# One PSUM pool with numbered accumulators for an MLP and a recurrence, and an accumulator of its own for the second transposed norm

## Chip, cores, metric

The kernel runs on one core of one Trainium2 chip. The metric is device time in microseconds (us), lower is better; beside it stands the span of the profiled execution, from its first to its last instruction.

## The reference, cut to what matters

Two computations on the same `x` (2048 rows of 512) are mixed by a gate that depends on the row:

```python
g = sigmoid((x * gate_w).sum(-1, keepdims=True))
a = A_ref(x, mem0, Wq, Wk, Wv, Wo, seg_len)   # 64 segments of 32 rows, in sequence: each attends to
                                              # 8 memory rows that the segment before it produced
b = gelu(layernorm(x) @ w1 + b1) @ w2 + b2    # MLP 512 -> 1376 -> 512, no recurrence
out = g * a + (1 - g) * b
```

## The kernel before

It computes the MLP first (until 99.7 us), keeps `(1 - g) * b` in on-chip memory, and then runs the 64 steps of the recurrence. The kernel uses eight banks of PSUM, the memory into which its matmuls write. An eviction copies a finished result out of its bank, on VectorE or ScalarE. The MLP takes the banks from two pools, the recurrence from a third that is opened when the MLP's pools are closed:

```python
mps = mlp.enter_context(tc.tile_pool(name="mps", bufs=1, space=PSUM))       # tp, hp x2, bp0..bp3: 7 banks
pools = {"ps": mlp.enter_context(tc.tile_pool(name="pre", bufs=1, space=PSUM)), ...}   # b5: 1 bank
def bank(k, shape, dtype=FP32):
    return pools["ps"].tile(shape, dtype, tag=f"b{k}", name=f"b{k}")

def norm_tr(T, y_sb):                              # transposes a normalized tile of x
    tp = mps.tile([P, KC, P], BF16, tag="tp", name="tp")
    for kc in range(KC):
        nc.tensor.transpose(tp[:, kc, :], y_sb[:, kc * P:(kc + 1) * P], ident[:])
    nc.vector.tensor_copy(out=yTs[blk][...], in_=tp[:])
# up(u): hp = mps.tile(tag="hp", bufs=2); GELU on ScalarE.   down(u): bp = mps.tile(tag=f"bp{T % 4}")
# ... cut ...
norm_tr(0, ys[0]); norm_tr(1, ys[1])               # the first two, one behind the other
for u in range(NBLK * FC):                         # 8 blocks of two x tiles, 11 chunks of F each
    ...                                            # up(u), down(u - 2), norms of the next block
    if fc == 2: c_act()                            # ScalarE evicts the odd tile of the block before
    if blk % 2 == 0:
        if fc in (2, 5, 6, 7): bn(...)             # statistics of later x tiles, VectorE
        if fc == 8: newton(...)                    # their inverse roots, VectorE
    if blk == 0 and fc in (9, 10): gates(fc - 9, fc - 8)   # x * gate_w, summed, tiles 0 and 1, VectorE
    if blk == 1 and fc == 0: gates2(0, 2)          # tanh on ScalarE
for a in pend: down(*a)
c_act()                                            # the last tile, T = 15
mlp.close()
# ... cut ...
pb = loop.enter_context(tc.tile_pool(name="pb", bufs=1, space=PSUM))        # b0..b7
pools.update(ps=pb, sb=cw, nTt=3, nside=2)
nc.scalar.activation(out=warm[:], in_=g_all[:, 0:1], func=ACTF.Exp)         # loads ScalarE's table
S_next = mask_mm()                                 # 4 matmuls into b7: the first work of the recurrence
```

All of it:

## Time and profile before

| | before |
|---|---|
| device time, median of the first 3 runs | 822.22 us (822.06 to 823.05) |
| profiled span | 821.1 us |
| TensorE busy | 793.0 us, 97% |
| TensorE idle in all | 28.1 us |
| of it in front of the second transposes | 0.52 us |
| of it in front of the first mask matmuls | 0.78 us |

In a timeline row stand the start, the duration, the engine, the source line, the operation, what it writes and reads, and in brackets how long the engine had been idle and what released it. Idle time counts for the end only if the chain of waits runs through it. The rows themselves are in the prediction.

### The profile page before, as it was taken

The numbers are of one execution on the slowest core, as the hardware profiler recorded it, in microseconds if no ns is written. First come the engines' busy times: TensorE is split into PE (matmuls) and PEld (weight loads), VectorE is DVE, ScalarE is ACT, GpSimd is POOL, SyncE is SP. The second block draws the span as 40 slices with busy tenths as digits, with TensorE's granted clock in tenths as the row PEclk, the third lists the DMA queues.
The fourth block names the chain that finished last, engine by engine and source line by source line (L and its number), as shares of the span: only waits on it lengthen the run. The fifth ranks groups of instructions, "written<-read, shape, count | busy, mean of one in ns | idle before, by whom it ended". The sixth has DMA issues, their size and how long they took to land.

```text
span 821.1 us, 48437 instructions
## 1 busy us (share of the span) xinstructions
PE 793.0 (97%) x22013; PEld 443.4 (54%) x22013; DVE 493.1 (60%) x1022; ACT 446.6 (54%) x1239; POOL 272.7 (33%) x624
## 2 busy tenths in 40 slices
PE   6999999999999999999999999999999999999986
PEld 3666545555555555555555555555555555555543
DVE  5764256565656666665666565666566565756554
ACT  3555445655555555555555645555565555565553
POOL 8100224242434243243424242423333242424220
PEclk9999999999999999999999999999999999999999
DMA  9791310000000010101010100101010101010000
GB/s 314 238 404 48 104 28 11 25 16 15 25 20 26 10 36 10 37 11 33 6 38 10 31 17 20 27 18 28 10 36 11 36 4 40 7 34 8 10 5 24
DMA packets 38357, 37.59 MB, mean 46 GB/s; under 512 B 13561, under 2 KB 36578, under 8 KB 36610
## 3 DMA queue, kind: packets, MB, share of 16 engines
q1 hardware_dynamic: 38018, 34.31, 12.6%
q8 instruction: 174, 2.85, 1.5%
q14 instruction: 37, 0.30, 0.1%
q0 software_dynamic: 128, 0.13, 0.1%
HBM read 26.03 MB, written 6.29 MB: 39 GB/s over the span
## 4 chain that ended last, share of the span: by engine, by line
PE 92%; DVE 4%; issue 1%; DMA 1%; SPq 1%; ACT 1%; DVEq 0%; ACTq 0%
PE b L211 33%; PE b L233 18%; PE b L222 16%; PE b L398 5%; PE hp L470 4%; PE bp L487 4%; PE b L360 3%; PE b L374 2%; PE b L365 2%; PE b L383 2%; PE b L403 1%; DVE R L692 1%; DMA Wo_sb<-in_A_x_dram 1%; DVE Pm L695 1%; PE b L387 0%
## 5 line engine op out<-in xcount | busy, mean ns | idle before, releaser
L217 DVE STREAM_TRANSPOSE Tt<-b 128x512 f32<-128x512 f32 (+1 forms) x384 | 225.6, 613 | 82.2 <-PE b L211 70.3
L211 PEld LDWEIGHTS <-hT 128*32 128x32 bf16 x5120 | 131.3, 97 | 108.2 <-DVE hT L721 23.5
L233 PE MATMUL b<-Wo_sb,UTT 128*32 128x512 bf16 (+1 forms) x2656 | 160.9, 378 | 1.3 <-ACT UTT L763 0.9
L222 PE MATMUL b<-Wv_sb,hT 128*32 128x512 bf16 x2048 | 141.8, 378 | 0.0
L211 PE MATMUL b<-Wq_sb,hT 128*32 128x512 bf16 x2048 | 133.3, 380 | 3.2 <-DVE hT L721 1.7
L211 PE MATMUL b<-Wk_sb,hT 128*32 128x256 bf16 (+1 forms) x3072 | 133.3, 308 | 0.0
L667 ACT CAST KT<-Tt 128x256 bf16<-128x256 f32 (+1 forms) x192 | 87.1, 476 | 53.6 <-DVE Tt L217 53.5
L620 POOL TENSOR_TENSOR Px<-E,R 128x256 bf16<-128x256 bf16 x63 | 42.5, 675 | 208.9 <-DVE R L704 208.9
L704 DVE RECIPROCAL R<-b 128x256 f32<-128x256 f32 x63 | 110.7, 1757 | 0.0
L667 POOL CAST QT<-Tt 128x512 bf16<-128x512 f32 x64 | 39.2, 613 | 187.1 <-DVE Tt L217 187.1
L233 PEld LDWEIGHTS <-UTT 128*32 128x32 bf16 x2656 | 64.4, 96 | 63.8 <-DVE UTT L703 12.2
L711 ACT CAST wsb<-b 128x512 bf16<-128x512 f32 x63 | 36.9, 586 | 111.2 <-PE b L233 111.2
L692 DVE RECIPROCAL R<-b 128x64 f32<-128x64 f32 x63 | 35.1, 557 | 78.4 <-PE b L360 78.4
L634 ACT CAST UTT<-b 128x256 bf16<-128x256 f32 x248 | 74.4, 386 | 9.7 <-PE b L403 7.5
L667 ACT CAST QT<-Tt 128x512 bf16<-128x512 f32 x64 | 39.6, 619 | 68.7 <-DVE Tt L217 68.7
L222 PEld LDWEIGHTS <-hT 128*32 128x32 bf16 x2048 | 49.4, 96 | 21.2
L475 ACT ACTIVATE hg<-hp,b_sb 128x256 bf16<-128x256 f32 x80 | 37.8, 474 | 39.9 <-PE hp L470 39.9
L721 DVE CAST hT<-b 128x32 bf16<-128x32 f32 x63 | 12.1, 191 | 79.0 <-PE b L365 79.0
L398 PEld LDWEIGHTS <-V 32*128 32x128 bf16 x4064 | 34.4, 91 | 45.6 <-DVE Pm L695 32.3
L470 PE MATMUL hp<-yT,w_sb 128*128 128x256 bf16 (+1 forms) x352 | 54.7, 281 | 2.2 <-DMA w_sb<-in_B_w_dram 0.9
L703 ACT CAST UTT<-b 128x64 bf16<-128x64 f32 x126 | 20.6, 215 | 66.1 <-PE b L403 66.1
L622 POOL TENSOR_TENSOR racc<-racc,R 128x320 f32<-128x320 f32 x63 | 54.9, 871 | 0.0
(131 smaller groups left out, 1056.5 us busy)
## 6 DMA issues: line engine op xcount, KB each, us to landing
Wv_sb<-in_A_Wv_dram SPq DMA_DIRECT2D x4, 1024.0 KB
Wq_sb<-in_A_Wq_dram SPq DMA_DIRECT2D x4, 1024.0 KB
Wk_sb<-in_A_Wk_dram SPq DMA_DIRECT2D x4, 1024.0 KB
Wo_sb<-in_A_Wo_dram SPq DMA_DIRECT2D x2, 2048.0 KB
vd<-vt SPq DMA_DIRECT2D x32, 128.0 KB
vs<-vd SPq DMA_DIRECT2D x256, 16.0 KB
out_dram<-o SPq DMA_DIRECT2D x15, 128.0 KB
Wo_sb<-in_A_x_dram SPq DMA_DIRECT2D x1, 1024.0 KB
```

The lines of the kernel that those rows point to most:

```text
L211: nc.tensor.matmul(bk[32 * j:32 * j + 32, 0:n], lhsT=G[:, kc, :], rhs=W5[t][:, kc, h0:h1, j, :], start=(kc == 0), stop=(kc == KC - 1), til ...
L217: nc.vector.transpose(out=Tt[:, 0:n], in_=bk[:, 0:n])
L222: nc.tensor.matmul(bk[32 * j:32 * j + 32, :], lhsT=G[:, kc, :], rhs=Wv5[:, kc, 4 * vb:4 * vb + 4, j, :], start=(kc == 0), stop=(kc == KC - ...
L233: nc.tensor.matmul(bk[32 * g:32 * g + 32, :], lhsT=ut[:, i, j, c0:c0 + 32], rhs=Wo_sb[:, 4 * i + j, d0:d1], start=(j == 0 and i < 4), stop ...
L398: nc.tensor.matmul(U[j][:, i, :], lhsT=V[q, i, :], rhs=Pt[q, i, c_main:c_main + n], start=(i == 0), stop=False, skip_group_check=True, til ...
L470: nc.tensor.matmul(hp[:rows, :], lhsT=w1_sb[:, kc, fc * P:fc * P + rows], rhs=yTs[blk][:, kc, :], start=(kc == 0), stop=(kc == KC - 1))
L620: nc.gpsimd.tensor_tensor(out=Px[:, :, 0:32], in0=E[:, :, 16:48], in1=Rr, op=ALU.mult)
L622: nc.gpsimd.tensor_tensor(out=racc[:], in0=racc[:], in1=R[:], op=ALU.add)
L634: nc.scalar.copy(out=UTT[T % 2][:, :, j, c0 + M:c0 + 40], in_=U[:])
L667: (nc.gpsimd.tensor_copy if bi == 2 else nc.scalar.copy)(out=dst, in_=Tv)
L692: nc.vector.reciprocal(out=R[:, 0:8 * NG].rearrange("p (i q) -> p i q", q=8), in_=sm[:])
L704: nc.vector.reciprocal(out=R[:, 8 * NG:].rearrange("p (i q) -> p i q", q=32), in_=sr)
```

## The change

The intent: one pool `pb` lives from the start to the end, and every PSUM tile is one of its numbered accumulators. `hp` becomes b0 and b1, `bp` becomes b2, b3, b4, b6, the side work stays b5, `tp` becomes b7. A tile then waits only for the last user of its own accumulator, not for a whole pool. The second transposed norm goes into b6, which nothing else needs so early, so it need not wait for the copy of the first.

```diff
+    pb = loop.enter_context(tc.tile_pool(name="pb", bufs=1, space=PSUM))
     mlp = ExitStack()
...
-    mps = mlp.enter_context(tc.tile_pool(name="mps", bufs=1, space=PSUM))
-    pools = {"ps": mlp.enter_context(tc.tile_pool(name="pre", bufs=1, space=PSUM)), "sb": mwork}
+    pools = {"sb": mwork}
...
     def bank(k, shape, dtype=FP32):
-        return pools["ps"].tile(shape, dtype, tag=f"b{k}", name=f"b{k}")
+        return pb.tile(shape, dtype, tag=f"b{k}", name=f"b{k}")
...
-    def norm_tr(T, y_sb):
+    def norm_tr(T, y_sb, k=7):
-        tp = mps.tile([P, KC, P], BF16, tag="tp", name="tp")
+        tp = bank(k, [P, KC, P], BF16)
...
-        hp = mps.tile([P, TB * P], FP32, tag="hp", bufs=2, name="hp")
+        hp = bank(u % 2, [P, TB * P])
...
-                bpt[T] = mps.tile([P, Dm], FP32, tag=f"bp{T % 4}", name="bp")
+                bpt[T] = bank((2, 3, 4, 6)[T % 4], [P, Dm])
...
-    norm_tr(1, ys[1])
+    norm_tr(1, ys[1], 6)
...
-    pb = loop.enter_context(tc.tile_pool(name="pb", bufs=1, space=PSUM))
-    pools.update(ps=pb, sb=cw, nTt=3, nside=2)
+    pools.update(sb=cw, nTt=3, nside=2)
```

## The prediction

> **What bounds the kernel now.** I read the page's busy shares first, then the chain of waits in order of time, then the timeline around the two places that the diff touches.
>
> ```profile
> PE 793.0 (97%) x22013; PEld 443.4 (54%) x22013; DVE 493.1 (60%) x1022; ACT 446.6 (54%) x1239; POOL 272.7 (33%) x624
> ...
> PE   6999999999999999999999999999999999999986
> ...
> PE 92%; DVE 4%; issue 1%; DMA 1%; SPq 1%; ACT 1%; DVEq 0%; ACTq 0%
> ```
>
> TensorE is busy for 97% of 821.1 us and carries 92% of the chain that ended last. The row of tenths falls under 9 only in the first slice (0 to 20.5 us) and at the very end. So a change can win only where TensorE stands still and something on the chain holds it; 28 us in all (821.1 - 793.0). Two of those gaps belong to code in the diff. The first is at the start, in the TensorE timeline:
>
> ```profile
> 5.66 0.60 PE L459 MATMUL tp<-ident,y 128*128 128x128 bf16 x4 [5.66 <-DVE y L452]
> 6.78 0.58 PE L459 MATMUL tp<-ident,y 128*128 128x128 bf16 x4 [0.52 <-DVE yT L460]
> 7.88 2.72 PE L470 MATMUL hp<-yT,w_sb 128*128 128x256 bf16 x12 [0.52 <-DVE yT L460]
> 10.39 1.06 PE L487 MATMUL bp<-w_sb,hg 128*128 128x512 bf16 x2
> 12.39 1.04 PE L470 MATMUL hp<-yT,w_sb 128*128 128x256 bf16 x4 [0.94 <-DMA w_sb<-in_B_w_dram]
> ```
>
> The second transposes wait 0.52 us for VectorE to copy the first ones out of the single tp buffer; the third row waits 0.52 us again. The last row waits for a weight transfer. The second gap is where the MLP ends and the recurrence begins, same view:
>
> ```profile
> 99.12 0.60 PE L487 MATMUL bp<-w_sb,hgl 97*128 97x512 bf16 x2
> 100.50 0.37 PE L374 MATMUL b<-MkA,ident 128*32 128x448 bf16 x4 [0.78 <-ACT c_all L495]
> 100.69 1.05 PE L211 MATMUL b<-Wq_sb,hT 128*32 128x512 bf16 x16
> ```
>
> The mask matmuls open the recurrence; their operands are long there, yet they wait 0.78 us until ScalarE has finished the MLP's last eviction. Whether a gap is on the chain, the chain of waits in order of time says:
>
> ```profile
> 8.04 8.09 DMA Wo_sb<-in_A_x_dram
> 16.15 0.70 DVE st L413
> ...
> 24.42 0.47 ACT hg L475
> 24.93 0.60 PE hp L470 x4
> ...
> 98.43 1.31 PE bp L487 x6
> 99.74 0.02 issue
> 99.76 0.70 ACT c_all L495
> 100.46 0.04 issue
> 100.50 0.37 PE b L374 x4
> ```
>
> TensorE enters the chain only at 24.93 us. Before that the chain is the transfer of x tiles (lands at 16.13), then VectorE statistics and gates in queue order, then ScalarE. So the first gap lies off the chain, the second lies on it.
>
> **What the Trainium skill says.** "PSUM — Partial Sum Buffer", section "PSUM bank collisions raise a hardware error": access to PSUM is to be guarded by semaphores per bank (and quadrant). That is why a new owner of a bank waits for the last reader of the old one, which is legitimate; but the wait at 100.50 us is wider: in the built program of before the mask's accumulator lies in bank 0, where the transposes' buffer was, while the evictions at 99.55 and 99.76 us read banks of the MLP's down-projection. The wait is that of a new pool for the whole old pool. "Perfetto Trace Analysis", "Matmuls": independent matmul groups should rotate through different banks so that one's eviction overlaps the next one's matmuls; both gaps here break that, and the trace agrees (0.52 and 0.78 us idle). "ScalarE: Activation LUTs", "What ACT_TABLE_LOAD costs": about 1283 ns for the load; the trace has 1.28 us at 100.51 us. "TensorE: Matmul & The Clock Gate", "What's actually happening": the array starts at half rate and is released after a free-running window of about 3.4 us of activity. The trace agrees in kind: four matmuls of 256 columns take 1.04 us at 12.39 us and 0.60 us from 15.73 us.
>
> **The change part by part.** I compared the two built programs instruction by instruction, line numbers and names set aside. All five engines have the same instructions in the same order (47,729 entries on TensorE), and SBUF addresses are equal. The only differences in waits are five, all on TensorE: the second transposes lose their wait for VectorE; the mask's weight load loses its wait for VectorE and the first mask matmul its wait for ScalarE; the first matmuls into b2 and into b4 in the first step gain a wait each for VectorE. Physical banks are permuted; each accumulator still has one of its own.
>
> (1) Second transposed norm. Both y tiles are ready at 5.19 + 0.73 = 5.92 us. Four cold transposes take about 0.45 us of issue (the weight-load row of that place: 0.45), so the second four can go at about 6.1 us in place of 6.78: 0.68 us earlier. VectorE copies them behind its first copy (6.30 + 0.42), from about 6.73 in place of 7.40; the up-projection starts at about 7.2 in place of 7.88. TensorE then reaches the weight wait at about 10.8 in place of 11.45, and the transfer still comes at 12.38: the 0.94 us wait becomes about 1.6 us. Even without that wait, the chain from 8.04 to 24.42 us holds no TensorE work, and TensorE idles 0.77 us before 24.93 us for ScalarE. Value to the end: 0.
>
> (2) The hand-over of the pools. Two 512-column matmuls issue in 0.43 us (elsewhere in the MLP such a pair is followed by the next group 0.43 us later: 93.92 to 94.35). The pair at 99.12 is therefore issued by 99.55, and the mask can go at 99.55 instead of 100.50: 0.95 us. In later steps the mask follows its predecessor with some 0.2 us of weight-load issue on the load side, about 0.05 of it seen by the matmuls, so 0.9 us.
>
> (3) Does it arrive? The table load for Exp starts at 100.51 us after the last eviction and, with the warm call, holds ScalarE until 101.81 + 0.20 = 102.01 us. The first query cast stands at 102.69, waiting for VectorE; 0.92 us earlier it would be ready at 101.77 and starts 0.24 us late at 102.01. It takes 0.62, so the second (ready at 103.40 - 0.92 = 102.48) starts at 102.63, 0.15 late; the next (104.59 - 0.92 = 103.67) finds ScalarE free since 103.25. The delay is gone before the scores (104.80 before), which waited for no cast anyway. GpSimd's query cast had 1.62 us of idle time ahead. VectorE's first block transpose would move from 101.94 to about 101.0, after the eviction that ends at 100.30.
>
> (4) The two new waits: b4's matmuls come 4 x 0.86 us after the first block's start at about 99.75, so at about 103.2; the last VectorE eviction ended at 100.30. Cost 0. The side accumulator b6 is free since 100.45 and is wanted at about 106.
>
> (5) The remaining 63 steps have the same instructions and waits and move as one block: no further gain or loss.
>
> Sum: 0 + 0.92 + 0 = 0.92 us; 822.22 - 0.92 = 821.3 us, and the profile's span 821.1 - 0.9 = 820.2.
>
> **The rivals.** (A) The start counts too: 0.68 + 0.92 = 1.6 us, 820.6. For it: TensorE really starts earlier, and may leave its half-rate state earlier. Against: the weight wait at 12.39, and the chain, which meets TensorE only at 24.93. (B) ScalarE's table load takes the place of the removed wait: if the first step hung on its casts, 0.24 us of 0.92 would be lost, or all of it if the table load delayed the chain; 821.5 to 822.2. For: it becomes the last thing to end. Against: 0.57 us of idle time ahead of the key cast at 104.59 absorbs it. (C) The clock release falls one 3.4 us window later because TensorE's idle stretch before 12.39 grows. That costs at most about half a window, 1.7 us, less the 0.77 us of slack at 24.93: 822.2. It varies from run to run whatever the kernel. (D) The word-by-word intent (one pool, numbered accumulators) suggests a freer recurrence, several per cent; but its 63 steps have unchanged waits, so I give it next to nothing.
>
> **Range and chances.** The three times of before lie within 822.06 to 823.05, about 1 us, as large as the effect; a median of three should scatter by some 0.5 us. With A at one side and B and C at the other: 820.4 to 822.4 us. Two per cent would be 16.4 us, over half of all TensorE's idle time: faster 0.005, same 0.99, slower 0.005.
>
> **What would show it.** Right: the transposes at about 6.1 us without a wait; the weight wait grown to about 1.6 us; the 24.93 us row where it was within 0.1 us; the mask at about 99.6 us without a wait; the first query cast behind the warm call; every later row of the recurrence earlier by a constant 0.9 us. Wrong: a TensorE row near 24.93 that moved with the start (A); a shift at 104 us that has shrunk by 110 us (B); half-rate matmuls lasting beyond 16 us (C); a shift that changes between 120 and 800 us (a step of the recurrence I took for unchanged).

## The result, and the profile after

| | before | after |
|---|---|---|
| median of 4 runs each | 822.63 us (822.06 to 823.24) | 821.70 us (821.08 to 822.29) |
| profiled span | 821.1 us | 820.5 us |
| TensorE busy | 793.0 us | 793.3 us |

The ratio is 0.9988, 95% interval 0.9971 to 1.0006. The interval holds 1: total times alone hardly show an effect of this size, and the traces have to. Line numbers after are one higher than before up to the hand-over.

The start, TensorE's timeline of the changed kernel:

```profile
5.62 1.03 PE L460 MATMUL b<-ident,y 128*128 128x128 bf16 x8 [5.62 <-DVE y L453]
7.16 2.72 PE L471 MATMUL b<-yT,w_sb 128*128 128x256 bf16 x12 [0.51 <-DVE yT L461]
...
11.91 1.03 PE L471 MATMUL b<-yT,w_sb 128*128 128x256 bf16 x4 [1.18 <-DMA w_sb<-in_B_w_dram]
```

The eight transposes are now one row without a wait in between, and the first up-projection starts at 7.16 in place of 7.88 us. Then the weight transfer stops TensorE as before, for 1.18 us where it had been 0.94.

The hand-over, same view:

```profile
99.09 0.60 PE L488 MATMUL b<-w_sb,hgl 97*128 97x512 bf16 x2
99.62 0.37 PE L375 MATMUL b<-MkA,ident 128*32 128x448 bf16 x4
99.82 1.04 PE L212 MATMUL b<-Wq_sb,hT 128*32 128x512 bf16 x16
```

The mask waits for nothing and starts 0.53 us after the last down-projection pair, where it had been 1.38 us (99.12 to 100.50).

The chain of waits in order of time (start, duration, piece):

```profile
7.86 8.24 DMA Wo_sb<-in_A_x_dram
...
24.38 0.47 ACT hg L476
...
24.89 0.60 PE b L471 x4
...
98.39 1.30 PE b L488 x6
99.69 0.30 PE b L375 x4
```

It still begins with the x transfer and still meets TensorE only at 24.89 us (24.93 before): the 0.72 us won at 7 us did not reach it. The eviction that stood between the down-projection and the mask is off the chain.

ScalarE's timeline at the hand-over:

```profile
100.47 1.28 ACT L606 ACT_TABLE_LOAD   x1
101.77 0.20 ACT L606 ACTIVATE warm<-g_all 128x1 f32<-128x1 f32 x1
101.88 0.60 ACT L667 CAST QT<-Tt 128x512 bf16<-128x512 f32 x1
102.52 0.62 ACT L667 CAST KT<-Tt 128x512 bf16<-128x512 f32 x1
103.71 0.75 ACT L667 CAST KT<-Tt 128x256 bf16<-128x256 f32 x2 [0.57 <-DVE Tt L218]
```

The first cast no longer waits for VectorE but comes right behind the table load; by the third row ScalarE has caught up and waits 0.57 us again.

### The profile page after: what moved, and what is told of

Same layout as the page of the kernel before. It is cut to its first block, busy times and chain, and to the rows that moved or that the text cites. A ratio compares the mean times of both kernels' runs of the same rounds, so it can differ in the third digit from the quotient of the medians.

```text
span 820.5 us, 48437 instructions
## 1 busy us (share of the span) xinstructions
PE 793.3 (97%) x22013; PEld 443.2 (54%) x22013; DVE 493.0 (60%) x1022; ACT 446.2 (54%) x1239; POOL 272.1 (33%) x624
## 4 chain that ended last, share of the span: by engine, by line
PE 93%; DVE 3%; DMA 1%; issue 1%; SPq 1%; ACT 1%; DVEq 0%; ACTq 0%
PE b L212 34%; PE b L234 18%; PE b L223 16%; PE b L399 5%; PE b L471 4%; PE b L488 4%; PE b L361 3%; PE b L375 2%; PE b L366 2%; PE b L384 2%; PE b L404 1%; DMA Wo_sb<-in_A_x_dram 1%; PE b L388 0%; DVE R L692 0%; DVE hT L721 0%
## 5 line engine op out<-in xcount | busy, mean ns | idle before, releaser
L476 ACT ACTIVATE hg<-b,b_sb 128x256 bf16<-128x256 f32 x80 | 37.7, 473 | 39.6 <-PE b L471 39.6
L471 PE MATMUL b<-yT,w_sb 128*128 128x256 bf16 (+1 forms) x352 | 54.7, 281 | 2.8 <-DMA w_sb<-in_B_w_dram 1.2
```

Source lines behind the costliest of these rows:

```text
L471: nc.tensor.matmul(hp[:rows, :], lhsT=w1_sb[:, kc, fc * P:fc * P + rows], rhs=yTs[blk][:, kc, :], start=(kc == 0), stop=(kc == KC - 1))
L476: nc.scalar.activation(out=hg_[:rows, :], in_=hp[:rows, :], func=ACTF.Gelu_apprx_tanh, bias=b1_sb[:rows, fc:fc + 1], scale=1.0)
```

## The experiments

Twelve kernels, all correct, in five rounds beside the kernel before; the first eight on one chip, the last four on another. For the partial kernels, the built programs were compared: `start_only` and `handover_only` differ from the kernel before in one and four waits of TensorE, `evict_b7` from the changed kernel in two, and in nothing else of the order. (In `evict_b7` the second of the two is for TensorE itself, which had long done.)

| run | median us (range) | ratio to before [95%] | mask starts at, us |
|---|---|---|---|
| before (first profile) | 822.22 | | 100.50 |
| after (first profile) | 821.70 | 0.9988 [0.9971, 1.0006] | 99.62 |
| after_again | 821.32 (821.12 to 822.76) | 0.9987 [0.9973, 1.0] | 99.54 |
| start_only | 823.02 (822.0 to 824.24) | 1.0002 [0.9988, 1.0015] | 100.60 |
| handover_only | 822.05 (821.01 to 822.16) | 0.9988 [0.9974, 1.0001] | 99.91 |
| evict_b7 | 822.91 (822.51 to 823.65) | 1.0004 [0.9991, 1.0018] | 100.57 |
| act_busy | 822.61 (821.95 to 822.99) | 0.9997 [0.9983, 1.001] | 99.55 |
| gates_early | 820.86 (819.9 to 821.42) | 0.9974 [0.996, 0.9988] | 97.67 |
| gates_split | 820.57 (820.3 to 820.85) | 0.9973 [0.9961, 0.9986] | 98.32 |
| gates_split_tp1 | 820.20 (819.75 to 822.33) | 0.9976 [0.9961, 0.999] | 98.29 |
| stats_late | 820.85 (820.2 to 823.22) | 0.998 [0.9966, 0.9993] | 101.28 |
| stats_late_tp1 | 820.72 (819.9 to 821.21) | 0.9977 [0.9963, 0.999] | 98.11 |
| late_split | 819.37 (819.05 to 819.55) | 0.9961 [0.9947, 0.9974] | 97.82 |
| late_split_tp1 | 819.46 (818.82 to 820.07) | 0.9962 [0.9948, 0.9976] | 97.61 |

The medians of before beside them were 822.59 (first four), 822.62 (second four) and 822.27 us (last four).

### Which of the two parts brings it: after_again, start_only, handover_only, evict_b7

Theory: only the hand-over is worth anything. Rivals: the start counts too; or the permuted banks do it and the wait does not matter.

`after_again` is the changed kernel unaltered, on the same chip as the three below.

> The changed kernel once more, on the same chip and in the same rounds as the three partial kernels. My theory (only the hand-over of the accumulators is worth anything): 0.9 us under the kernel before; mask matmuls near 99.6 us against 100.5. Rival (the start counts too): 1.5 us under it.

`start_only` is the kernel before, with the start part alone:

```diff
-    def norm_tr(T, y_sb):
+    def norm_tr(T, y_sb, k=None):
-        tp = mps.tile([P, KC, P], BF16, tag="tp", name="tp")
+        tp = mps.tile([P, KC, P], BF16, tag="tp", name="tp") if k is None else bank(k, [P, KC, P], BF16)
-    norm_tr(1, ys[1])
+    norm_tr(1, ys[1], 5)
```

> The kernel before with the second transposed norm in the spare bank b5 and the old pools otherwise; the built program differs from that of before in one wait. My theory: transposes and first up-projection 0.6 to 0.7 us earlier, the wait for the weight transfer longer by what is won, the TensorE row near 24.9 us and the mask at 100.5 us where they were, total time within 0.1 us of before (0.0). Rival (the start counts): mask near 99.9 and total 0.6 us less.

`handover_only` is the changed kernel without the start part:

```diff
-    norm_tr(1, ys[1], 6)
+    norm_tr(1, ys[1])
```

> The changed kernel with both first transposed norms in b7 again; four waits differ from before, all at the hand-over. My theory: second transposes wait 0.5 us as before, mask near 99.6 us, total 0.9 us less than before, equal to the changed kernel. Rival (the start counts): 0.3 us, with the remaining 0.6 lost again.

`evict_b7` is the changed kernel with the last MLP tile in the accumulator that the mask takes first:

```diff
-                bpt[T] = bank((2, 3, 4, 6)[T % 4], [P, Dm])
+                bpt[T] = bank(7 if T == NT - 1 else (2, 3, 4, 6)[T % 4], [P, Dm])
```

> The changed kernel with the last MLP tile (T = 15) accumulated in b7, the bank that the mask takes first, so that the mask has a true dependence on the last eviction; one wait (mask for ScalarE) comes back. My theory: mask again at about 100.5 us behind the eviction that ends at 100.45, gain of 0.9 us gone, total as before (0.0 +- 0.2 us). Rival (the permuted banks or the single pool itself bring the gain, the wait does not matter): total stays 0.9 us under before.

TensorE's timeline of `start_only`:

```profile
5.57 0.61 PE L459 MATMUL tp<-ident,y 128*128 128x128 bf16 x4 [5.57 <-DVE y L452]
5.97 0.64 PE L459 MATMUL b<-ident,y 128*128 128x128 bf16 x4
7.12 2.72 PE L470 MATMUL hp<-yT,w_sb 128*128 128x256 bf16 x12 [0.52 <-DVE yT L460]
...
12.45 0.61 PE L470 MATMUL hp<-yT,w_sb 128*128 128x256 bf16 x4 [1.75 <-DMA w_sb<-in_B_w_dram]
...
25.02 0.60 PE L470 MATMUL hp<-yT,w_sb 128*128 128x256 bf16 x4 [1.55 <-ACT hg L475]
...
100.60 0.37 PE L374 MATMUL b<-MkA,ident 128*32 128x448 bf16 x4 [0.78 <-ACT c_all L495]
```

The transposes and the up-projection are 0.7 us earlier, and both later waits are longer: 1.75 us for the weights (0.94 before), 1.55 us for ScalarE (0.77 before). The mask waits 0.78 us as ever.

TensorE's timeline of `evict_b7` at the hand-over:

```profile
99.20 0.60 PE L488 MATMUL b<-w_sb,hgl 97*128 97x512 bf16 x2
100.57 0.37 PE L375 MATMUL b<-MkA,ident 128*32 128x448 bf16 x4 [0.78 <-ACT c_all L496]
```

With the single pool and the numbered accumulators all in place, a true dependence on the last eviction brings the 0.78 us back, and the gain is gone (1.0004 to before).

Six traces read at four points tell the parts apart more sharply than any total. S is VectorE's first statistics row behind the x transfer, P the first TensorE row on the chain, M the first mask matmul; all in us:

| profile | S | idle before P | P | M | P - S | M - P |
|---|---|---|---|---|---|---|
| before | 16.15 | 0.77 | 24.93 | 100.50 | 8.78 | 75.57 |
| start_only | 16.27 | 1.55 | 25.02 | 100.60 | 8.75 | 75.58 |
| evict_b7 | 16.23 | 1.58 | 25.00 | 100.57 | 8.77 | 75.57 |
| after | 16.12 | 1.14 | 24.89 | 99.62 | 8.77 | 74.73 |
| after_again | 16.04 | 1.58 | 24.81 | 99.54 | 8.77 | 74.73 |
| handover_only | 16.44 | 0.51 | 25.18 | 99.91 | 8.74 | 74.73 |

P follows S by 8.74 to 8.78 us, whatever TensorE does meanwhile; what TensorE wins or loses before P only changes its idle time there. M - P has two values: 75.57 to 75.58 us where the mask waits for the eviction, 74.73 us where it does not. The hand-over is worth 75.57 - 74.73 = 0.84 us, the start 0.00, and the differences left over between runs (16.04 to 16.44) are those of the x transfer's landing.

The same six profiles settle the clock's part. In `before`, `after` and `handover_only` four matmuls of 256 columns still took 1.03 to 1.04 us in the row behind the weight wait, in `start_only`, `after_again` and `evict_b7` 0.61 us: the array had been released earlier. It changed the idle time before P (0.51 to 1.14 us against 1.55 to 1.58), and P not at all.

### How much slack ScalarE has at the hand-over: act_busy

The rival that the table load takes the wait's place was tested by loading ScalarE more:

```diff
     nc.scalar.activation(out=warm[:], in_=g_all[:, 0:1], func=ACTF.Exp)
+    for T in range(2):
+        wl = cw.tile([P, Dm], BF16, tag="wl", bufs=1, name="wl")
+        nc.scalar.activation(out=wl[:], in_=c_all[:, T, :], func=ACTF.Exp)
```

> The changed kernel with two ScalarE activations of 128x512 (0.6 to 0.7 us each, result unused) added behind the table load at the hand-over: the load on ScalarE there more than an estimate of its slack (0.57 us ahead of the key cast, plus what TensorE has ahead of the scores). My theory: first query cast 1.2 to 1.4 us later, the key casts late by 0.6 to 0.8 us, the scores late by 0.2 to 0.8 us and the total as much longer than the changed kernel. Rival (ScalarE's table load already holds the first step): the scores and the total later by the full 1.2 to 1.4 us. If ScalarE has still more slack: no change.

ScalarE's timeline of `act_busy`:

```profile
101.81 1.27 ACT L609 ACTIVATE wl<-c_all 128x512 bf16<-128x512 bf16 x2
102.99 0.60 ACT L670 CAST QT<-Tt 128x512 bf16<-128x512 f32 x1
103.50 1.53 ACT L670 CAST KT<-Tt 128x512 bf16<-128x512 f32 x3
```

Counted from the mask, which stood at 99.55 us, the first query cast is 1.18 us later (3.44 us in place of 101.88 - 99.62 = 2.26), the three key casts run without a pause, and the 0.57 us of idle time is used up. The second step's mask came at 110.17 us: 10.62 us behind the first, where it is 9.97 in the changed kernel (99.62 to 109.59). So 1.18 us of load cost 0.65 us, and about 0.53 us was slack behind the table load. (The medians differ by more, 822.61 against 821.32 us; that is the scatter of totals treated below.) The table load is not what the first step hangs on, but there is little more than half a microsecond to spare.

### What covers the start: gates_early, gates_split, gates_split_tp1

If the start is set by the chain from the x transfer, then taking VectorE's gates out of it must move P. VectorE idles 3.62 us before that transfer lands (trace of `before`), and the gates of tiles 0 and 1 fit in there:

```diff
-        if blk == 0 and fc in (9, 10):
-            gates(fc - 9, fc - 8)
+        if blk == 0 and fc == 1:
+            gates(0, 2)
```

> The changed kernel with the two gate reductions of tiles 0 and 1 moved from the end of the first MLP block (up-projection chunks 9 and 10) to chunk 1, into VectorE's idle stretch of 3.6 us before the x tiles land at 16.1 us. My theory (the start is set by the chain x transfer, VectorE in queue order, ScalarE's tanh, then its next GELU): the tanh no longer waits, TensorE's idle time of 0.77 us before 24.9 us goes, that row and all later ones 0.7 to 0.8 us earlier, total 0.7 to 0.8 us under the changed kernel, 1.6 us under before. Rival (the weight transfer at 12 us or the half-rate clock sets the start): under 0.2 us.

TensorE's timeline of `gates_early`:

```profile
11.97 0.61 PE L471 MATMUL b<-yT,w_sb 128*128 128x256 bf16 x4 [1.19 <-DMA w_sb<-in_B_w_dram]
...
17.51 0.38 PE L460 MATMUL b<-ident,y 128*128 128x128 bf16 x4 [0.80 <-DVE yT L461]
...
97.67 0.37 PE L375 MATMUL b<-MkA,ident 128*32 128x448 bf16 x4
```

The wait near 24.9 us is gone, the chain now meets TensorE at 17.51 us, and the mask is 1.95 us earlier than in the first profile of the changed kernel, of which 0.2 is an earlier landing (VectorE's statistics at 15.91 us against 16.12). The theory is confirmed and the rival (under 0.2 us) refuted, but the size was wrong: I had taken the 0.77 us of idle time from the profile of before, in which TensorE reached P late because it ran at half rate until 15.7 us. Here it ran at full rate from 11.97 us and could use more: `after_again`, as early at full rate, idles 1.58 us before P. (Some 0.15 us of the gain stays unaccounted for.) Of this the medians of the totals show 0.46 us (821.32 to 820.86); why less is told in the section on totals and traces.

Next, the weight transfer that stops TensorE near 12 us, cut in two, with and without the start part:

```diff
-    nc.sync.dma_start(w1_sb[:, :, 3 * P:F], w1_src[:, :, 3 * P:F])
+    nc.sync.dma_start(w1_sb[:, :, 3 * P:5 * P], w1_src[:, :, 3 * P:5 * P])
+    nc.sync.dma_start(w1_sb[:, :, 5 * P:F], w1_src[:, :, 5 * P:F])
```

> As the one with the gates moved, and the weight transfer that TensorE waits for near 12 us cut in two (chunks 3 and 4 first, 256 KB, then the rest). My theory: the wait before 12 us shrinks from 1.2 us to under 0.5, and the total falls by up to 1 us more, unless VectorE's statistics of the x tile that lands at 16.1 us then hold the transposes. Rival: the first piece lands no earlier than the whole, nothing changes.

> As the one before (gates moved, transfer cut in two), but the second transposed norm back in b7 behind the first one's copy. If the early start of the transposes was worth nothing only because the transfer and the VectorE chain covered it, this one is now slower than its partner, by up to 0.6 us, seen in the TensorE rows at 25 us. If the start's value is nil for another reason, or the transfer still covers it, both are equal within 0.1 us there.

The weight wait fell to 0.28 us, yet the mask came at 98.32 us, 0.65 us later than in `gates_early`. The chains of waits tell why. `gates_early`:

```profile
7.78 8.11 DMA Wo_sb<-in_A_x_dram
```

`gates_split`:

```profile
9.74 6.80 DMA Wo_sb<-in_A_x_dram
```

One more transfer in the queue ahead of the x tiles, and they land at 9.74 + 6.80 = 16.54 us in place of 15.89: 0.65 us later, exactly what the mask lost. TensorE's next transposes then wait 1.76 us for VectorE; the expectation had named this obstacle. The partner without the start part landed the tiles at 16.49 us, waits 1.25 us at the same place and had its mask at 98.29. So the start part was again worth nothing; the x transfer was the cover.

### With that cover gone too: stats_late, stats_late_tp1, late_split, late_split_tp1

VectorE stood still for the x transfer with work behind it that TensorE needs (the copy at 17.5 us). In the first block, the statistics were moved behind the transposes:

```diff
+    BNF = ((7, 8, 9, 10), (2, 5, 6, 7))
-            if fc in (2, 5, 6, 7) and T1 + 2 < NT:
-                bn(T1 + 2 + (2, 5, 6, 7).index(fc) )
-            if fc == 8 and T1 + 2 < NT:
+            if fc in BNF[blk > 0] and T1 + 2 < NT:
+                bn(T1 + 2 + BNF[blk > 0].index(fc))
+            if fc == (8 if blk else 10) and T1 + 2 < NT:
```

`stats_late` is `gates_early` with this, `late_split` is `gates_split` with this; `_tp1` has the second transposed norm back in b7.

> The kernel with the gates moved, and in the first MLP block the statistics of tiles 4 to 7 moved behind the second transposed pair (chunks 7 to 10 in place of 2, 5, 6, 7; their root at 10 in place of 8), so that VectorE does not stand before the x transfer with work that TensorE needs. My theory (after the gates moved, TensorE waited 0.80 us at 17.5 us for VectorE behind that transfer): the wait goes, the mask comes 0.5 to 0.9 us earlier than with the gates moved alone (97.67), if the array's clock is released as early; released one window later it costs up to 1.7 us at the mask now, as nothing covers it. Total 819.5 to 821. Rival: another VectorE result holds TensorE, mask near 97.7 again.

> As the one before, with the second transposed norm back in b7. The wait for the weight transfer near 12 us (1.2 us with the early transposes) still covers the start: the rows from 12.4 us on are equal within 0.1 us once the landing of that transfer and the time of the clock's release are taken off. Rival: 0.7 us slower.

`stats_late` missed its expectation: in its profile the mask came at 101.28 us, later even than before. TensorE's timelines show one cause in each kernel. `stats_late`:

```profile
12.53 1.03 PE L471 MATMUL b<-yT,w_sb 128*128 128x256 bf16 x4 [1.51 <-DMA w_sb<-in_B_w_dram]
...
15.91 1.06 PE L471 MATMUL b<-yT,w_sb 128*128 128x256 bf16 x4
```

`stats_late_tp1`:

```profile
12.17 0.61 PE L471 MATMUL b<-yT,w_sb 128*128 128x256 bf16 x4 [0.77 <-DMA w_sb<-in_B_w_dram]
...
24.50 0.60 PE L471 MATMUL b<-yT,w_sb 128*128 128x256 bf16 x4 [0.42 <-ACT hg L476]
...
27.95 0.38 PE L460 MATMUL b<-ident,y 128*128 128x128 bf16 x4 [0.46 <-DVE yT L461]
```

With the start part, this execution stayed at half rate until about 18 us; its partner ran at full rate from 12.17 us. Nothing covers that now, so it costs the whole 3.17 us at the mask (101.28 - 98.11), 0.36 of it a later landing of the weights; the other 2.81 us are more than the 1.7 us that the expectation allowed. Those are two profiles of one execution each. The slow profile belongs to the slowest run of its kernel (823.22 us); the other four were 820.2 to 821.67, and the medians of the two kernels are 820.85 and 820.72 us. When the clock is released, not the start part, is what differs.

The partner was not held by the clock, and still its mask (98.11 us) is behind that of `gates_early` (97.67). The 0.80 us at 17.51 us are gone, but the statistics now keep VectorE busy from 17.5 us on, the chain of waits runs through them, and TensorE waits 0.42 us at 24.50 and 0.46 us at 27.95 us for results behind them. So the rival was right here: another VectorE result holds TensorE, and moving the statistics brought nothing at the mask.

> Gates and statistics moved, and the weight transfer in two pieces. Now neither the transfer, nor the x tiles, nor the gates cover the start; TensorE should run from its first up-projection at 7.1 us to the mask with under 0.5 us of waits. Mask 0.5 to 1.0 us earlier than without the cut, total 819 to 820.5.

> As the one before, with the second transposed norm back in b7: here the start part of the change should for the first time be worth something. If its value was only covered: mask 0.3 to 0.7 us later than in its partner (0.7 less what remains of the weight wait), apart from the clock's release. If its value is nil for another reason: equal.

TensorE's timeline of `late_split`:

```profile
15.08 0.59 PE L489 MATMUL b<-w_sb,hg 128*128 128x512 bf16 x2 [0.38 <-DMA w_sb<-in_B_w_dram]
```

and of `late_split_tp1`:

```profile
14.91 0.59 PE L489 MATMUL b<-w_sb,hg 128*128 128x512 bf16 x2 [0.43 <-DMA w_sb<-in_B_w_dram]
```

I had expected the start part to be worth 0.3 to 0.7 us here. It was not: the next transfer, the second piece of the down-projection's weights, stops both kernels (0.38 and 0.43 us) and lands at 15.08 and 14.91 us; the masks (97.82 and 97.61) differ in the same direction by about as much, in favour of the kernel without the start part. The totals are equal (819.37 and 819.46 us). The expected "under 0.5 us of waits" was missed as well: TensorE in `late_split` waits 0.46 us at 10.39 and 0.38 us at 15.08 for weights, and 0.50 us at 24.21 and 0.46 us at 27.66 behind the moved statistics, 1.80 us in all. In no arrangement that I ran did the start part reach the end: each time another transfer lay in front of TensorE.

`late_split` has the lowest time found: 819.37 us, 0.9961 of before, and the changed kernel was 0.9988 and 0.9987 of it. These two were run neither in the same rounds nor on the same chip, and their intervals (up to 0.9974, and from 0.9971 or 0.9973) overlap a little. That its start is better than that of `gates_early` is not shown: its mask is no earlier (97.82 against 97.67 us), and the lower total (spans of 817.6 and 819.1 us) comes from behind the mask, most of it from the stops treated next.

### Why totals and traces differ

Comparing the 64 mask rows of `after` with those of `before`, the shift is -0.88 us at the first, -0.80 at the eleventh, -1.29 near the 25th, and -0.73 at the last. It jumps at single places, and TensorE's timeline of the changed kernel shows such a place:

```profile
663.52 0.62 PE L212 MATMUL b<-Wk_sb,GL 128*32 128x512 bf16 x8 [0.44 <-issue]
```

"issue" is idle time that no wait in the profile accounts for. The place is the same in other traces, only the length differs: this row starts 0.70 us after the start of the row ahead of it, in `before` (at 664.31 us) 0.41 us, in `late_split` (at 660.87 us) 0.12 us.

Laid over each other matmul by matmul from the first mask on, the fourteen traces depart from their median by more than 0.12 us at a dozen places only. Seven of these come back from kernel to kernel, in steps 6, 11, 16, 24, 34, 47 and 52; the distance to the matmul ahead is there between 0.01 and 0.61 us. Together the seven take 0.66 to 2.06 us, and without them the recurrence takes 713.59 to 713.93 us in twelve of the fourteen traces (714.32 in `act_busy`, with its added load, and 714.14 in `late_split_tp1`, with one more stop). They do not belong to the change: the unaltered changed kernel has 1.78 us of them in `after` and 1.25 in `after_again`. `gates_early` has 2.06 and `late_split` 0.91. In `before` and `after` they nearly cancel (1.80 and 1.78); of the 0.88 us at the first mask, 0.73 are left at the last and 0.6 at the end of the span.

What causes the stops stays open, as no run was made for it. One hint: in the built program the seven places are whole multiples of 256 TensorE instructions apart (3328 between the first three), and the profile's instruction queue moved 174 packets for 48437 recorded instructions, an estimated 278 for each packet. That points to the loading of instructions.

## Why the prediction was right

The time was 821.70 us against 821.3 predicted, inside 820.4 to 822.4. That the number came so close is partly luck: the median of before moved from 822.22 to 822.63 us with its fourth run, and the interval of the ratio holds 1. The traces test the steps:

1. **The start is worth nothing to the end.** Right, for the reason given: P - S is 8.74 to 8.78 us with and without it. The second transposes started at 5.97 us in `start_only` (about 6.1 predicted) and the up-projection at 7.16 us after the change (7.2). The weight wait became 1.18 us rather than 1.6, because the transfer landed 0.5 us earlier in that profile; in `start_only`, where it landed at 12.45 us, it was 1.75. (The weight-load row that the prediction reads for four transposes holds five loads; the second four started 0.40 us behind the first.)
2. **The hand-over is worth 0.92 us.** Right in mechanism, the term a little large: 0.84 us measured. The mask follows the last pair by 0.53 us; I had put its issue slot at 0.43 and added 0.03 to 0.05 (the text says 0.9, the sum takes 0.92). `evict_b7` shows that the wait itself was the cause, not the permuted banks or the single pool. One reading of the skill does not fit: only the first gap breaks its advice to rotate through banks. At the second the banks already differed, as the prediction itself says; the wait was the pool's.
3. **The gain arrives.** Right: the cast came behind the table load, ScalarE had caught up by 103.71 us, and the second mask kept the shift (109.59 against 110.47, 0.88). `act_busy` puts the slack at about 0.53 us.
4. **The two new waits cost nothing.** Right: the matmuls into b2 and b4 follow each other in the changed kernel at 0.86 to 0.87 us a block without an idle entry.
5. **The other 63 steps move as one block.** Not confirmed by the pair of traces: the shift wandered between -0.73 and -1.29 us, which the prediction had named as a sign against it. What moved it were the stops of varying length that all fourteen traces share, not a step that the change altered.

Of the rivals in the prediction, A (the start counts) and B (the table load takes the wait's place) are refuted by the runs. C (the clock's release) was bounded too tightly at 1.7 us less 0.77. In the changed kernel nothing of it showed, because 0.5 to 1.6 us of idle time before P took it up; `stats_late` shows that a late release can cost nearly 3 us once nothing covers it. D (a freer recurrence) did not occur: TensorE's busy time and its waits in the steps are as before.

## What to carry to other kernels

Two stages that share PSUM should share one pool with accumulators by name, so that the first matmul of the second stage waits for the last reader of its own bank and not for the first stage's last eviction; here that was worth 0.84 us, once. Before taking a wait away, look in the chain of waits whether it meets that engine at all: 0.7 us at the start of this kernel was worth nothing, because the chain ran through a transfer and VectorE, and behind each cover that was removed the next transfer or the next VectorE result came to light. For effects under one part in a thousand compare fixed points of the traces, such as the landing of a transfer and the first matmul behind it, rather than totals.

## What the Trainium skill lacked or had wrong

- "ScalarE: Activation LUTs", "What ACT_TABLE_LOAD costs", puts a switch of sets at about 2.66 us: 1283 ns of load and about 1380 ns of drain. At the hand-over the trace has the load at 1.28 us, but the eviction ahead of it ends at 100.41 us, the load starts at 100.47 and the next activation at 101.77: 1.36 us for the whole switch, with no drain of that length.
- "TensorE: Matmul & The Clock Gate", "What's actually happening", gives about 3.4 us of first activity at half rate, with a transition that varies by about 0.5 us, though it also says that the number of slow matmuls changes from run to run. Here the first matmul came at 5.6 to 6.1 us, and full rate was seen from 9.91 us (`evict_b7`), 15.73 us (`before`) and about 18 us (`stats_late`), though the last had been computing without a wait since 12.53 us. The spread is about 8 us; for the unaltered changed kernel it is about 3 us (15.30 us in `after`, 12.07 at the latest in `after_again`).
- No page gives a size for stops of TensorE without any wait that come at the same places in every trace here and vary in length: seven places, up to 0.6 us each, 0.66 to 2.06 us in all.
